# Attention by clusters, then a gated feed-forward layer: a new table of places for the kernel's 2390 tasks

## The chip, the cores and the metric

The kernel runs on one core of a Trainium2 chip. The metric is the device time of one execution in microseconds, lower is better. Names of engines: PE is the matrix engine (TensorE), DVE the vector engine, ACT the scalar engine, POOL the GpSimd engine, SP the engine that does little else than issue DMAs. PEld stands for loading weights into the matrix engine, which overlaps its matmuls.

## The reference: what is computed

Four batches of eight heads, 768 positions, 64 elements per head. Each query and each key belongs to one of 16 clusters of its head, and only pairs of the same cluster attend to each other. The result of all heads goes, as 3072 tokens of 512 elements, through a feed-forward layer with a sigmoid gate, 1536 wide inside:

```python
q_assign = np.argmax(np.einsum('bhsd,hcd->bhsc', q_n, c_n), axis=-1)
k_assign = np.argmax(np.einsum('bhsd,hcd->bhsc', k_n, c_n), axis=-1)
mask = q_assign[:, :, :, None] == k_assign[:, :, None, :]
scores = scale * np.matmul(q, k.transpose(0, 1, 3, 2))
scores = np.where(mask, scores, -1000000000.0)
...
gate = 1.0 / (1.0 + np.exp(-(x @ w_gate)))
val = x @ w_val
return (gate * val @ w_out).astype(np.float32)
```

The inputs and the output are float32.

## The kernel before

**Work.** Heads go in pairs, (batch, pair) from (0,0) to (3,3). For each pair, q and k (tiles `nat`) are loaded, transposed on PE into PSUM (L723) or by DVE (L701), and copied to SBUF as `t32` (L683 on DVE, others on ACT). POOL casts `t32` to fp16 tiles `even` and `odd` (L756). A group of fp32 matmuls of 16 instructions (`scored`, L793 and its like) compares `t32` with the centroids; from it DVE makes a one-hot matrix of each position's cluster, and small transposes (L680) put it as 16 further rows beneath `even` and `odd`. A score matmul (L1113) thus contracts over 80 rows, and the 16 extra ones are the cluster mask. Several score matmuls fill two PSUM banks, ACT takes the exponential of both at once (L1137, into `es`), and value products (L1164) follow. Their 65th column is the sum of a row: DVE takes its reciprocal (L1189) and multiplies (L1194, into `xn`). The result is transposed into the layer's input `x`, either on PE with a cast by DVE (L1202, L1218) or by a transposing DMA from SP (L1222).

**The layer.** A block of tokens goes through the two projections (L1505), ACT's sigmoid, and the gated product on DVE (L1684, into `hT`). From the second batch on the projections are in part replaced by seven products of halves in place of eight (L1583), which need sums of weights (L1486) and evacuations with additions. The output projection is done by seven products as well (L1374), with sums of activations on DVE (L1344) and sums of the weights `wo` (L1272 to L1277). These sums are made once, after the three loads of `wo`, which POOL issues.

**The order.** Nothing runs in the order in which it is written. The program first records 2390 tasks: 1048 for PE, 584 for DVE, 453 for ACT, 107 for POOL, 198 for SP. A task is a small group of instructions of one engine with its dependencies, an assumed duration, and the buffers it takes. `Order.schedule` then plays them through: on each engine, among the tasks that could start within 0.02 us of the earliest one, it takes that with the lowest place (`due`, from the table `PLACES`):

```python
first = min(c[0] for c in cand)
start, t = min(
    (c for c in cand if c[0] <= first + 0.02), key=lambda c: (c[1].due, c[0])
)
```

For DMAs it assumes the time from issue to landing in the table `LANDINGS`. In the same pass it deals out the buffers: `ring` is the pool of eight PSUM banks, and a task gets one of those that are free when the planner believes it to start. So the places set the order of each engine's instructions and also which bank a product lands in, hence for which evacuation it waits. On the chip the engines then run that fixed order, with semaphores between them. A DMA of POOL is issued only when fewer than eight of POOL's are under way; these loads and SP's transposes share the core's 16 DMA engines.

Around the places shown below: `prepare_pair` (L885) records the transposes, copies and casts of a pair, `attend` (L1091) scores to norms, `sum_weights` (L1254) the sums over `wo`, `feed` (L1492) the projections. Their code is the same in both kernels.

Of the kernel before, what the change touches and what calls it, by code (L numbers as in the profile page):

```python
# [17 lines left out]
0 1 10 13 16 2 3 9 12 11 6 15 17 19 20 32 36 4 8 5 14 18 21 23 27 75 68 31 37 40 99 94 43 47 52 215 128 58 163 194  # L18
105 119 221 207 277 259 475 252 501 7 22 24 30 26 25 29 35 41 28 33 38 50 34 39 44 46 42 48 53 57 61 64 65 70 77 86
82 79 45 51 49 55 54 59 56 62 63 112 78 87 76 90 101 113 138 136 144 158 133 124 139 88 97 96 107 106 118 114 129  # L20
131 156 137 147 135 151 160 169 214 191 179 204 185 196 199 117 122 130 140 132 145 150 183 171 229 182 198 195 219
227 235 248 242 257 270 261 275 268 104 110 116 192 172 200 184 253 206 265 228 279 250 287 254 290 285 299 288 305
267 286 295 300 316 323 318 361 368 380 399 330 348 373 403 413 420 407 427 439 433 454 446 336 381 363 342 349 431
441 371 355 448 488 424 521 554 529 535 512 517 539 543 594 598 639 643 558 568 574 605 648 678 647 653 657 663 670
673 654 660 664 675 677 693 685 709 716 695 704 713 787 66 67 69 73 85 71 72 74 80 92 81 83 84 89 100 91 93 95 98
123 142 149 152 102 103 108 153 109 111 115 154 120 121 126 157 125 127 134 159 141 143 155 170 146 148 161 181 189
209 216 162 164 165 166 167 168 173 217 174 175 176 177 178 180 186 218 225 232 237 187 188 190 193 197 238 201 202
203 205 208 239 210 211 212 213 220 241 246 251 255 222 223 224 226 230 256 231 233 234 236 240 258 243 244 245 247
249 266 273 284 310 319 260 262 263 264 269 298 271 272 274 276 278 301 280 281 282 283 289 311 317 321 332 338 459
466 515 506 344 352 347 365 360 370 372 385 353 359 383 392 421 432 426 443 401 410 405 425 434 453 465 472 444 457  # L30
494 499 473 486 485 492 500 509 528 534 536 542 538 546 508 526 516 530 552 560 556 567 291 292 293 294 296 297 302
333 303 304 306 307 308 309 313 334 341 346 350 314 315 320 351 325 327 331 364 328 329 337 366 339 340 345 393 357
358 362 394 367 369 374 397 402 406 462 375 376 377 378 379 382 384 412 386 387 388 389 390 391 395 415 422 428 477
398 400 404 442 408 411 416 450 417 418 423 455 429 430 436 458 437 440 445 460 449 452 461 476 483 487 495 463 467
468 469 470 471 474 493 478 479 480 481 482 484 489 503 507 510 519 523 490 491 496 520 497 498 502 522 504 505 511
525 513 514 518 541 524 527 531 545 532 533 537 547 551 553 557 562 572 577 624 619 570 576 604 618 591 627 626 637
635 642 640 649 622 631 652 668 575 581 579 623 613 621 617 628 655 674 683 690 661 672 671 680 676 687 705 714 692
719 701 724 666 694 686 697 711 723 717 729 573 580 587 612 615 616 620 630 645 578 583 592 602 708 722 727 728 732
# [1783 lines left out]
```

## Time and profile before

| | |
|---|---|
| median of 3 runs | 311.12 us (310.98 to 311.52) |
| the profiled execution | 310.43 us, its span 308.6 us |
| busy: PE, ACT, DVE, POOL | 299.5, 260.1, 248.5, 79.2 us |
| granted clock of PE | 1.00 |

The span goes from the first to the last instruction; the execution is 1.8 us longer. A row of the timeline gives the start of a run of like instructions, the time from the first one's start to the last one's end, engine, line, operation, the tiles that are written and read, the shape, the count, and in brackets how long the engine was idle before it and what ended that. Matmuls are pipelined: 128x512 ones start 0.22 us apart though each lasts longer. The lines of code in the profile after will be higher by one than those before, since the new table is a line longer.

### The profile page before, as it was taken

To read this page: it belongs to the slowest core of one execution; us is meant where nothing else is said; L and a number is where in the kernel's file an instruction comes from. 1 tells how busy PE (TensorE), PEld (TensorE's weight loads), DVE (VectorE), ACT (ScalarE), POOL (GpSimd) and SP (SyncE) were. 2 spreads that over 40 slices of the span, in tenths; PEclk is the share of its full clock that TensorE was granted. 3 is DMA by queue.
4 is the path that set the end of the run, shared out by engine and by line. 5 is a ranking of instruction groups with operands and counts; after the bars stand their busy time and mean duration, and the time that the engine had idled before them with its cause. 6 is when DMAs were issued, how large, how long until landed. Compare 5 with 4: busy or idle time off the path is not lost.

```text
span 308.6 us, 8896 instructions
## 1 busy us (share of the span) xinstructions
PE 299.5 (97%) x3491; PEld 237.5 (77%) x3491; DVE 248.5 (81%) x604; ACT 260.1 (84%) x449; POOL 79.2 (26%) x112
## 2 busy tenths in 40 slices
PE   8999999989999999999999999999999999999995
PEld 3667588744468688977998779886998889878974
DVE  4999996798796696889679979979786839864993
ACT  4798899975539899999999988999999998995841
POOL 4998738751022014600001211370000000010000
PEclk9999999999999999999999999999999999999999
DMA  6999999999457389920376564894210120051003
GB/s 216 376 283 165 177 225 158 149 154 130 76 90 145 71 180 152 150 36 15 81 121 120 97 106 106 184 136 32 68 21 35 29 81 34 3 96 70 0 3 136
DMA packets 97833, 34.79 MB, mean 113 GB/s; under 512 B 83152, under 2 KB 93568, under 8 KB 97792
## 3 DMA queue, kind: packets, MB, share of 16 engines
q1 hardware_dynamic: 72192, 24.57, 35.6%
q0 software_dynamic: 24880, 8.92, 28.9%
q10 hardware_dynamic: 720, 0.75, 0.7%
q8 instruction: 27, 0.44, 0.6%
q14 instruction: 14, 0.11, 0.1%
HBM read 28.87 MB, written 6.29 MB: 114 GB/s over the span
## 4 chain that ended last, share of the span: by engine, by line
PE 71%; ACT 13%; DVE 8%; DMA 4%; issue 2%; ACTq 0%; DVEq 0%
PE ring L1583 19%; PE ring L1374 17%; PE ring L1113 14%; PE ring L1505 10%; PE ring L1164 8%; ACT es L1137 7%; DMA x<-xn 3%; PE ring L793 2%; ACT nat L1621 2%; ACT nat L1602 2%; DVE even L680 2%; DVE t L683 1%; DVE odd L680 1%; DMA out<-in_centroids_dram 1%; ACT p L1602 1%
## 5 line engine op out<-in xcount | busy, mean ns | idle before, releaser
L1137 ACT ACTIVATE es<-ring,nbias 128x768 f16<-128x768 f32 (+1 forms) x189 | 168.9, 939 | 16.4 <-PE ring L1113 10.1
L1164 PEld LDWEIGHTS <-es 128*128 128x128 f16 x1152 | 50.8, 97 | 9.5 <-ACT es L1137 0.8
L1164 PE MATMUL ring<-vp,es 128*128 128x65 f16 x1152 | 55.7, 193 | 0.2 <-ACT es L1137 0.2
L1614 DVE TENSOR_TENSOR nat<-ring,nat 128x384 f32<-128x384 f32 x68 | 36.9, 552 | 17.5 <-PE ring L1583 9.5
L756 POOL CAST even<-t 128x768 f16<-128x768 f32 x24 | 20.9, 876 | 113.9 <-DVE t L701 49.0
L1621 ACT ACTIVATE nat<-nat 128x384 f32<-128x384 f32 x68 | 38.4, 582 | 2.4 <-DVE nat L1614 2.3
L1583 PEld LDWEIGHTS <-wss 128*128 128x128 f16 x408 | 34.5, 98 | 2.2
L1602 ACT COPY nat<-ring 128x384 f32<-128x384 f32 x68 | 34.4, 521 | 2.1 <-PE ring L1583 1.1
L1583 PE MATMUL ring<-nat,wv 128*128 128x192 f16 x272 | 32.9, 246 | 0.0
L1583 PE MATMUL ring<-x,wg 128*128 128x192 f16 x272 | 32.6, 246 | 0.0
L1583 PE MATMUL ring<-nat,wss 128*128 128x192 f16 x272 | 31.9, 246 | 0.0
L1374 PEld LDWEIGHTS <-hT 128*128 128x128 f16 x294 | 27.4, 97 | 5.7 <-DVE hT L1630 0.4
L1374 PE MATMUL ring<-wo,hT 128*128 128x256 f16 x216 | 29.0, 272 | 0.1
L1113 PE MATMUL ring<-even 80*128 80x384 f16 (+2 forms) x120 | 26.4, 294 | 1.1 <-ACT es L1137 0.5
L1113 PE MATMUL ring<-even,odd 80*128 80x384 f16 (+2 forms) x120 | 26.4, 293 | 0.5 <-DVE t L683 0.4
L1113 PE MATMUL ring<-odd 80*128 80x384 f16 x96 | 26.2, 325 | 0.0
L1113 PE MATMUL ring<-odd,even 80*128 80x384 f16 x96 | 25.8, 326 | 0.3 <-ACT es L1137 0.2
L1583 PEld LDWEIGHTS <-wv 128*128 128x128 f16 x272 | 23.5, 97 | 2.4
L1113 PEld LDWEIGHTS <-odd 80*128 80x128 f16 x216 | 18.7, 98 | 7.5 <-issue 4.4
L1113 PEld LDWEIGHTS <-even 80*128 80x128 f16 x216 | 19.0, 98 | 7.0 <-issue 3.2
L1583 PEld LDWEIGHTS <-wg 128*128 128x128 f16 x272 | 23.1, 98 | 1.5
L1505 PE MATMUL ring<-x,wg 128*128 128x256 f16 (+2 forms) x112 | 22.6, 325 | 1.0 <-DMA x<-xn 1.0
(120 smaller groups left out, 519.6 us busy)
## 6 DMA issues: line engine op xcount, KB each, us to landing
out_dram<-out SPq DMA_DIRECT2D x22, 256.0 KB, 2.3
nat<-in_k_dram SPq DMA_DIRECT2D x32, 96.0 KB, 2.9
nat<-in_q_dram SPq DMA_DIRECT2D x32, 96.0 KB, 3.0
odd<-even SPq DMA_DIRECT2D x12, 192.0 KB, 4.2
vp<-in_v_dram POOLq DMA_DIRECT2D x24, 96.0 KB, 5.1
nat<-in_k_dram SPq DMA_DIRECT2D x5, 384.0 KB, 7.2
nat<-in_q_dram SPq DMA_DIRECT2D x5, 384.0 KB, 6.1
nat<-in_v_dram SPq DMA_DIRECT2D x4, 384.0 KB, 7.2
```

The lines of the kernel that those rows point to most:

```text
L680: nc.vector.transpose(to.bitcast(FP), of.bitcast(FP))
L756: nc.gpsimd.tensor_copy(t[:, NM[nm], cols], t32[p, nm].tile[:, cols])
L793: nc.tensor.matmul(out=ps[32 * g : 32 * g + 32, half, :QB], lhsT=cblk[:, 2 * p + half, :], rhs=t32[p, nm].tile[:, half * QB : (half + 1) * ...
L1113: nc.tensor.matmul(out=to, lhsT=kb.tile[0:80, 0, e * QB + j // 2 * 128 : e * QB + (j // 2 + 1) * 128], rhs=qb_.tile[0:80, 1, e * QB + c0 * ...
L1137: i = nc.scalar.activation(to, of, AF.Exp, bias=nbias, scale=D ** -0.5 if quarters(b, p) else scale,).ins
L1164: nc.tensor.matmul(out=av.tile[:, g : g + D + 1], lhsT=es.tile[:, i * N + c * 128 : i * N + (c + 1) * 128], rhs=vp[:, e, j, :], start=firs ...
L1374: nc.tensor.matmul(out=ps[:, lo:hi], lhsT=left_()[:, i], rhs=right(i)[:, lo:hi], start=new and i == 0, stop=i == NFC // 2 - 1, skip_group_ ...
L1505: nc.tensor.matmul(out=ps[:, :N], lhsT=ws[fc // FPG][:, dcc, fc % FPG, :], rhs=xb.tile[:, dcc, :N], start=(dcc == 0), stop=(dcc == NDC - 1),)
L1583: nc.tensor.matmul(out=ps[:, f], lhsT=w_[:, d, f], rhs=x_()[:, d], start=new and not (f or d), stop=d == 1, skip_group_check=True,)
L1602: nc.scalar.copy(held(i), bank(r_))
L1614: lambda: nc.vector.tensor_tensor(held(i), bank(r_), held(i), ALU.add), deps,
L1621: lambda: nc.scalar.activation(held(i), held(i), AF.Tanh, scale=0.5), [m], due_ffn(work), lat=0.16,
```

## The change

Two tables of numbers have other values: `PLACES` and `LANDINGS`. All code is the same, and so are the 2390 tasks, what each computes and what it depends on. Of the places 1889 differ, by 5.7 on average and at most by 106; of the 254 landings some 45 differ by more than 0.3 us.

```diff
--- before.py
+++ after.py
@@ -15,115 +15,116 @@
 PLACES = """
-0 1 10 13 16 2 3 9 12 11 6 15 17 19 20 32 36 4 8 5 14 18 21 23 27 75 68 31 37 40 99 94 43 47 52 215 128 58 163 194
-105 119 221 207 277 259 475 252 501 7 22 24 30 26 25 29 35 41 28 33 38 50 34 39 44 46 42 48 53 57 61 64 65 70 77 86
...
+0 1 9 2 16 3 5 10 11 13 14 15 17 19 20 32 36 4 8 6 12 18 21 23 27 92 97 31 37 40 101 115 43 47 52 165 169 58 178 184
+107 121 225 233 263 268 495 255 502 7 22 24 26 30 25 29 35 41 28 33 38 46 34 39 44 50 42 48 53 57 61 64 65 70 76 78
...
 """
 
 LANDINGS = """
-2.6 3.45 4.13 3.7 4.2 3.45 3.88 4.31 4.74 5.17 5.6 6.03 6.46 6.89 7.1 8.68 11.77 8.87 10.7 15.58 12.84 9.47 10.5
...
+2.6 3.45 4.13 3.7 4.2 3.45 3.88 4.31 4.74 5.17 5.6 6.03 6.46 6.89 7.1 8.677 11.409 7.348 9.688 13.473 16.613 9.04
...
```

(Each table goes on for many lines; they are all numbers of this kind.) What follows shows how instructions move. On PE 410 of 1048 tasks stand at the same position as before, on DVE 243 of 584, on ACT 304 of 453, on POOL 46 of 107, on SP 81 of 198. The largest shift on an engine is 25 tasks on PE, 16 on DVE, 6 on ACT, 8 on POOL and 13 on SP.

**The last pair of the first batch: DVE.** `ohf0` is the one-hot matrix of pair (0,3), `even3` and `odd3` the operands of its scores; the copies into `t320` to `t323` empty the banks of fp32 transposes of a later pair. Before:

```order
L680 STREAM_TRANSPOSE even3_77<-ohf0_92 32x192
L1194 TENSOR_TENSOR xn3_105<-ring_121,rr0_99 128x256
L683 TENSOR_SCALAR t320_70<-ring_121 128x384
L680 STREAM_TRANSPOSE odd3_83<-ohf0_92 32x192
L680 STREAM_TRANSPOSE even3_77<-ohf0_92 32x192
L683 TENSOR_SCALAR t321_71<-ring_121 128x384
L680 STREAM_TRANSPOSE even3_77<-ohf0_92 32x192
L1189 RECIPROCAL rr1_100<-ring_121 128x4
L680 STREAM_TRANSPOSE odd3_83<-ohf0_92 32x192
L683 TENSOR_SCALAR t321_71<-ring_121 128x384
L1194 TENSOR_TENSOR xn0_102<-ring_121,rr1_100 128x256
L683 TENSOR_SCALAR t322_72<-ring_121 128x384 x2
```

and with the change, from the first of the small transposes on:

```order
L681 STREAM_TRANSPOSE even3_77<-ohf0_92 32x192
L1190 RECIPROCAL rr0_99<-ring_121 128x4
L681 STREAM_TRANSPOSE even3_77<-ohf0_92 32x192
L1195 TENSOR_TENSOR xn3_105<-ring_121,rr0_99 128x256
L681 STREAM_TRANSPOSE odd3_83<-ohf0_92 32x192
L681 STREAM_TRANSPOSE even3_77<-ohf0_92 32x192 x2
L681 STREAM_TRANSPOSE odd3_83<-ohf0_92 32x192
L684 TENSOR_SCALAR t320_70<-ring_121 128x384
L1190 RECIPROCAL rr1_100<-ring_121 128x4
L684 TENSOR_SCALAR t320_70<-ring_121 128x384
L1195 TENSOR_TENSOR xn0_102<-ring_121,rr1_100 128x256
L684 TENSOR_SCALAR t321_71<-ring_121 128x384 x2
```

The six small transposes now stand ahead of all copies; the first copy into `t320`, formerly further ahead, is behind them too.

**The same place on PE.** L723 is the group of transposes that those copies empty; the scores with `even3` and `odd3` are the last of the pair. Before:

```order
L1113 MATMUL ring_121<-even3_77 128x256
L1113 LDWEIGHTS even3_77
L1113 MATMUL ring_121<-even3_77 128x256
L1113 LDWEIGHTS odd3_83
L1113 MATMUL ring_121<-even3_77,odd3_83 128x256
L1113 LDWEIGHTS odd3_83
L1113 MATMUL ring_121<-even3_77,odd3_83 128x256
L1113 LDWEIGHTS odd3_83
L1113 MATMUL ring_121<-even3_77,odd3_83 128x256
L723 MATMUL ring_121<-ident_124,nat3_64 128x128 x6
L1113 LDWEIGHTS even1_75
L1113 MATMUL ring_121<-even1_75 128x128
```

and with the change:

```order
L1203 LDWEIGHTS xn0_102
L1203 MATMUL ring_121<-ident16_125,xn0_102 128x128
L1203 LDWEIGHTS xn0_102
L1203 MATMUL ring_121<-ident16_125,xn0_102 128x128
L724 MATMUL ring_121<-ident_124,nat3_64 128x128 x3
L1114 LDWEIGHTS even3_77
L1114 MATMUL ring_121<-even3_77 128x256
L1114 LDWEIGHTS odd3_83
L1114 MATMUL ring_121<-even3_77,odd3_83 128x256
L1114 LDWEIGHTS odd3_83
L1114 MATMUL ring_121<-even3_77,odd3_83 128x256
L1114 LDWEIGHTS odd3_83
```

The last four scores of the pair now stand behind a turn of `xn0` and the last three transposes of `nat3`, for which the planner takes the bank that the second copy into `t321` empties. Before, the transposes stood behind these scores.

**Loads: POOL.** `wo0` and `wo2` are two of the three tiles of the output weights, `vp` the values of a pair, `nat` the quarters of a q or k. Before:

```order
L440 DMA nat3_64<-in_k_dram 32x24x32
L440 DMA nat5_66<-in_q_dram 32x24x32 x2
L440 DMA nat3_64<-in_k_dram 32x24x32
L440 DMA vp4_144<-in_v_dram 128x6x64 x2
L440 DMA wo0_136<-in_moe_w_out_dram 128x4x512
L440 DMA nat3_64<-in_k_dram 32x24x32
L440 DMA wo2_138<-in_moe_w_out_dram 128x4x512
L440 DMA vp0_140<-in_v_dram 128x6x64 x2
```

and with the change:

```order
L441 DMA vp4_144<-in_v_dram 128x6x64 x2
L441 DMA nat4_65<-in_k_dram 32x24x32 x3
L441 DMA nat5_66<-in_q_dram 32x24x32 x3
L441 DMA nat3_64<-in_k_dram 32x24x32 x3
L441 DMA vp0_140<-in_v_dram 128x6x64 x2
L441 DMA wo0_136<-in_moe_w_out_dram 128x4x512
L441 DMA wo2_138<-in_moe_w_out_dram 128x4x512
```

`vp0` now stands ahead of both weight tiles instead of behind them, and `vp4` further ahead of them than before.

**Transposing DMAs: SP.** Before:

```order
L1222 DMA_TRANSPOSE x1_107<-xn2_104 128x1x128
L440 DMA even5_79<-oht0_86 16x768
L440 DMA even4_78<-oht0_86 16x768 x2
L440 DMA even5_79<-oht0_86 16x768
L440 DMA odd4_84<-oht0_86 16x768 x2
L440 DMA odd5_85<-oht0_86 16x768 x2
L1222 DMA_TRANSPOSE x1_107<-xn3_105 128x3x128
L1222 DMA_TRANSPOSE x1_107<-xn0_102 128x1x128
L1222 DMA_TRANSPOSE x1_107<-xn1_103 128x3x128
```

and with the change:

```order
L1223 DMA_TRANSPOSE x1_107<-xn2_104 128x1x128
L1223 DMA_TRANSPOSE x1_107<-xn3_105 128x3x128
L441 DMA even4_78<-oht0_86 16x768 x2
L1223 DMA_TRANSPOSE x1_107<-xn0_102 128x1x128
L441 DMA even5_79<-oht0_86 16x768 x2
L441 DMA odd4_84<-oht0_86 16x768 x2
L441 DMA odd5_85<-oht0_86 16x768 x2
L1223 DMA_TRANSPOSE x1_107<-xn1_103 128x3x128
```

Two of the transposes into `x1` have moved ahead of most of the eight small DMAs; the last one stays behind them.

**The sums over the output weights: DVE.** Before:

```order
L701 STREAM_TRANSPOSE t322_72<-nat3_64 128x384 x2
L1344 TENSOR_TENSOR s120_116<-hT0_108,s110_115 128x768
L1189 RECIPROCAL rr0_99<-ring_121 128x6
L1194 TENSOR_TENSOR xn0_102<-ring_121,rr0_99 128x384
L1275 TENSOR_TENSOR nat7_68<-wo0_136,nat6_67 128x512
L1275 TENSOR_TENSOR nat7_68<-wo1_137,nat6_67 128x512
L1275 TENSOR_TENSOR nat7_68<-wo2_138,nat6_67 128x512
L1684 SCALAR_TENSOR_TENSOR hT1_109<-gt0_110,ring_121 128x512
L1277 TENSOR_TENSOR nat8_69<-wo0_136,nat7_68 128x512
L1684 SCALAR_TENSOR_TENSOR hT1_109<-gt1_111,ring_121 128x512
L1486 TENSOR_TENSOR wv1_134<-wg1_131,wv1_134 128x2x256
L1684 SCALAR_TENSOR_TENSOR hT1_109<-gt0_110,ring_121 128x512
```

and with the change:

```order
L1685 SCALAR_TENSOR_TENSOR hT1_109<-gt0_110,ring_121 128x512
L1273 TENSOR_TENSOR nat6_67<-wo1_137 128x512
L1274 TENSOR_TENSOR wo1_137<-wo1_137 128x2x256
L1273 TENSOR_TENSOR nat6_67<-wo2_138 128x512
L1274 TENSOR_TENSOR wo2_138<-wo2_138 128x2x256
L1276 TENSOR_TENSOR nat7_68<-wo0_136,nat6_67 128x512
L1276 TENSOR_TENSOR nat7_68<-wo1_137,nat6_67 128x512
L1276 TENSOR_TENSOR nat7_68<-wo2_138,nat6_67 128x512
L1278 TENSOR_TENSOR nat8_69<-wo0_136,nat7_68 128x512
L1278 TENSOR_TENSOR nat8_69<-wo1_137,nat7_68 128x512
L1278 TENSOR_TENSOR nat8_69<-wo2_138,nat7_68 128x512
L1685 SCALAR_TENSOR_TENSOR hT1_109<-gt1_111,ring_121 128x512
```

The nine instructions over `wo0` to `wo2` now stand in one row between two gated products into `hT1`, without the sums and the copy-transposes (`L1344`, `L701`) that stood between them.

Elsewhere tasks of PE, DVE and ACT trade places with neighbours. One such place is near the middle of the program, where six matmuls of the output projection (L1374) now stand ahead of a score that they followed.

205 rows, old and new, of tables (LANDINGS, PLACES) are left out of this document.

## The prediction

> **What bounds the kernel now.** I read the page first, then busy time by stretches, and then the engines' timelines wherever TensorE stood still. The page:
>
> ```profile
> span 308.6 us, 8896 instructions
> PE 299.5 (97%) x3491; PEld 237.5 (77%) x3491; DVE 248.5 (81%) x604; ACT 260.1 (84%) x449; POOL 79.2 (26%) x112
> PE 71%; ACT 13%; DVE 8%; DMA 4%; issue 2%; ACTq 0%; DVEq 0%
> ```
>
> PE is busy 97% of the span and carries 71% of the chain of waits. No instruction is removed here, so only time in which PE waits can be won, and any new wait is lost. The stretches tell where that time is (columns: us, then busy us and instruction count of PE, PEld, DVE, ACT and POOL, the granted clock, the DMA share, GB/s):
>
> ```profile
> 26.50:33.00 6.50, 5.51 (x77) 4.02 (x76) 6.12 (x17) 5.20 (x6) 3.99 (x6) 1.00 1.36 113
> 36.00:62.00 26.00, 25.48 (x338) 20.15 (x330) 20.97 (x58) 24.42 (x38) 17.58 (x24) 1.00 1.26 183
> 60.00:64.00 4.00, 2.98 (x29) 1.51 (x27) 3.72 (x6) 2.77 (x5) 3.08 (x4) 1.00 1.60 175
> 64.00:145.00 81.00, 81.00 (x869) 57.62 (x868) 66.70 (x154) 65.54 (x107) 17.50 (x21) 1.00 0.79 108
> ```
>
> PE lacks 1.0 us of work in 26.5 to 33, 1.0 us in 60 to 64, and nothing in 64 to 145. So the change decides itself at three places: the last pair of the first group (27 to 36 us), the weight loads and transposes around 50 to 70 us, and one wait at 145 us. Everywhere else PE is dense: a shuffle there can cost and hardly win.
>
> **Place 1: copies behind transposes, 27 to 36 us.** DVE feeds PE here, and its timeline shows in which order:
>
> ```profile
> 27.68 0.37 DVE L680 STREAM_TRANSPOSE even<-ohf 32x192 f32<-32x192 f32 x1
> 29.03 0.55 DVE L683 TENSOR_SCALAR t<-ring 128x384 f32<-128x384 f32 x1
> 30.41 0.56 DVE L683 TENSOR_SCALAR t<-ring 128x384 f32<-128x384 f32 x1
> 32.01 0.56 DVE L683 TENSOR_SCALAR t<-ring 128x384 f32<-128x384 f32 x1
> 32.60 0.42 DVE L1194 TENSOR_TENSOR xn<-ring,rr 128x256 f16<-128x256 f32 x1
> 32.94 1.94 DVE L683 TENSOR_SCALAR t<-ring 128x384 f32<-128x384 f32 x4
> ```
>
> Copies (L683, 0.55 us) empty the banks of PE's fp32 transposes; the small transposes (L680, 0.37 us) make the operands of the scores. Today they alternate. The changed order has all six L680 first, then the copies. Up to the second copy into t321 DVE has the same set of tasks behind it as today up to the norm at 32.60, which ends at 33.02. DVE is busy 6.12 of 6.50 us in this stretch, so that copy ends at about 33.1, whatever the order. On PE and ACT:
>
> ```profile
> 31.02 0.38 PE L1113 MATMUL ring<-even,odd 80*128 80x256 f16 x2 [0.44 <-DVE t L683]
> 32.04 0.50 PE L1113 MATMUL ring<-even,odd 80*128 80x256 f16 x3
> 32.63 1.00 PE L723 MATMUL ring<-ident,nat 128*128 128x128 f32 x6
> 34.99 0.49 PE L1113 MATMUL ring<-odd,even 80*128 80x384 f16 x2
> 35.41 1.50 PE L793 MATMUL ring<-t,cblk 128*32 128x384 f32 x16
> 30.44 1.11 ACT L1137 ACTIVATE es<-ring,nbias 128x1024 f16<-128x1024 f32 x1 [0.95 <-PE ring L1113]
> 31.91 4.61 ACT L1137 ACTIVATE es<-ring,nbias 128x1024 f16<-128x1024 f32 x5 [0.35 <-PE ring L1113]
> ```
>
> Today the pair's last scores are issued by 32.4, and the second exponential of the row of five takes them at about 32.9 (31.91 + 1.0). The third starts at 34.0 and ends at 34.9; at 34.99 PE goes on with the scores that need its bank, and the cluster scores (L793) follow at 35.41. In the new order those last four scores stand behind three L723 transposes, for which the planner dealt the bank that the second t321 copy empties. So: 33.1 + 0.06 for the semaphore + three transposes at 0.14 (0.84 us from 32.63 to the next group, for six) + four scores at 0.11 and 0.16 more until the last has drained = 34.15 for the exponential. That is 1.2 later than 32.9. The next exponential and the bank follow by the same amount, so L793 starts at about 36.5 instead of 35.41: **+1.1 us**. Behind it PE is dense (25.48 of 26.00 us in 36 to 62), so it isn't won back. Bounds: +0.5 if the lead of a few tenths that the new order has from 12 to 28 us lets the copies end before 32.6; +1.5 if every one of the copies waits for PE's transposes in turn.
>
> **Place 2: the x transpose and the weights of the last layer, 50 to 70 us.**
>
> ```profile
> 61.07 0.60 PE L1505 MATMUL ring<-x,wg 128*128 128x512 f16 x2
> 62.69 1.47 PE L1505 MATMUL ring<-x,wg 128*128 128x512 f16 x6 [1.02 <-DMA x<-xn]
> 50.83 4.01 SPq L1222 DMA_TRANSPOSE x<-xn  x3
> 51.96 0.78 POOL L440 DMA_DIRECT2D wo<-in_moe_w_out_dram  x1
> 53.43 0.87 POOL L440 DMA_DIRECT2D wo<-in_moe_w_out_dram  x1
> 54.18 1.65 POOL L440 DMA_DIRECT2D vp<-in_v_dram  x2
> x<-xn SPq DMA_TRANSPOSE x1, 9.2
> wo<-in_moe_w_out_dram POOLq DMA_DIRECT2D x2, 512.0 KB, 9.4
> DMA to landing us min/median/max: 8.1/9.4/10.8
> DMA to landing us min/median/max: 11.2/11.4/11.6
> DMA to landing us min/median/max: 2.7/2.7/2.7
> ```
>
> (The last five: the transpose issued last, the two wo loads in the stretch 51 to 54, their own landings, those of the two vp loads from 54.18 on, and, for comparison, a transpose issued at 91.9.) The transpose issued at 53.4 lands at 62.6 and releases PE: 62.69 − 61.07 − 2 × 0.22 (the x6 group's spacing) = 1.18 us lost. Issue plus landing gives wo 51.96 + 8.1 = 60.1 and 53.43 + 10.8 = 64.2, vp 54.18 + 11.2 = 65.4 and about 55.0 + 11.6 = 66.6: things land in the order of issue, across both queues, while the backlog lasts. One vp therefore costs 1.2 us, and one wo, from the landing before it at about 57.1, at most 2.9.
>
> The change issues vp ahead of both wo, and two of three x transposes ahead of SP's eight small moves. The last transpose then has no wo ahead of it and one vp more: 62.6 − 2.9 + 1.2 = 60.9; with both vp ahead 62.1. PE would want it at 61.07 − 0.7 (work moved behind it) + 0.4 (two matmuls) + 1.1 (place 1) = 61.9. The wait goes: **−1.18 us**, bound −0.6 if x lands at 62.5. By the Trainium skill ("DMA: Bandwidth & Descriptors", section "Queues, rings and completion order") each DMA engine takes turns between the queues it has work for, a packet at a time; by that the SP transpose would not stand behind POOL's loads at all. The 9.2 us against 2.7 speak against it, though not finally: that reading is rival 3.
>
> The price: the two wo land later, at about 60.1 + 2 × 1.2 + 1.3 (a quarter of nat, the last transpose) = 63.8 and 64.2 + 2.4 = 66.6. DVE sums over them (L1272 to L1277) hold back what is behind them in the queue:
>
> ```profile
> 61.05 1.87 DVE L1272 TENSOR_TENSOR nat<-wo 128x512 f16<-128x512 f16 x1
> 62.95 0.42 DVE L1273 TENSOR_TENSOR wo<-wo 128x512 f16<-128x512 f16 x1
> 68.37 1.08 DVE L1275 TENSOR_TENSOR nat<-wo,nat 128x512 f16<-128x512 f16 x3
> 69.38 0.68 DVE L1684 SCALAR_TENSOR_TENSOR hT<-gt,ring 128x512 f16<-128x512 f32 x1
> 70.31 0.68 DVE L1684 SCALAR_TENSOR_TENSOR hT<-gt,ring 128x512 f16<-128x512 f32 x1
> ```
>
> In the new order the first gated product (L1684) stands behind the two sums of the first wo: 63.8 + 0.8 = 64.6, and, with the rows that come before it in time, 65.5. The second stands behind everything: 66.6 + 0.8 (the last pair of sums) + 6 × 0.34 (three L1275 take 1.08) = 69.4, and ends at 70.1. PE asks for the banks that these two empty at about 66 and 69.5 (two scores of batch 1 that the planner put onto them): 0 to 0.3, and 0.2 to 0.6: **+0.5 us**. Bounds: 0, if the loads drain while the queue is not full (PE then never asks too early), and +1.3, if the first L1272 takes its 1.87 us beside POOL's casts again and the sums follow 0.8 later.
>
> **Place 3: 145 us.**
>
> ```profile
> 145.42 0.32 PE L1113 MATMUL ring<-even 80*128 80x384 f16 x1 [0.19 <-ACT es L1137]
> ```
>
> This score waited for ACT; six matmuls of the output layer (L1374) now stand ahead of it. They fill the gap of 0.35 us (0.19 idle, and the fill and drain around it): **−0.35**; 0 if ACT then is behind at the next score too.
>
> **All else** (over a thousand tasks moved by up to 25 places on PE, 16 on DVE, 6 on ACT) I price at 0: in 64 to 145 us PE already has 81.00 of 81.00, and the banks' releases have a stage of slack. The cover is ACT's and DVE's idle time there (65.54 and 66.70 of 81): if an order asks a bank one task too early, it costs one evacuation, 0.4 to 0.7 us. Bounds ±0.6.
>
> **Sum:** 1.1 − 1.18 + 0.5 − 0.35 = +0.07 us. The profiled execution took 310.43 us (1.8 of it around its span of 308.6) and the runs' median is 311.12, 0.7 above it; the sum is made on the profile, and put on the median it gives **311.2 us**.
>
> **The rivals.**
>
> 1. *Slower: DVE's queue head.* Sums that wait for wo block the gated products, so PE stalls at 66 and 69.5 by the full +1.3, and place 1 costs +1.5. 311.12 + 1.5 + 1.3 − 1.18 = 312.7. For it: at 62 to 70 DVE has hardly any idle time (3.72 of 4.00). Against: a wo has landed in 8.1 us. It decides once the second wo lands after 66.9.
> 2. *Faster: the start loses little and the gains are all real.* Place 1 +0.5, wait for x gone, wo in time, 145 us gained: 311.12 + 0.5 − 1.18 − 0.35 = 310.1. For it: the new order is ahead by some tenths before 28 us. Against: DVE has 0.4 us of idle time in 26.5 to 33.
> 3. *The x transpose isn't held back by what is issued before it* but by its own queue and the load on the engines. It then lands at about 62.6 as today. PE, asking at 61.9, still loses 0.7: 311.12 + 1.1 − 0.5 + 0.5 − 0.35 = 311.9. For it: the transpose's 9.2 us and the loads' 8.1 to 10.8 are alike, which a shared backlog gives in any case. Against: landings in order of issue over two queues.
>
> **Chances.** Forecast 0.44 (own range 310.4 to 311.9), rival 1 0.17, rival 2 0.25, rival 3 0.14. A measurement of this kernel tells a change from none at about 0.2%, 0.62 us here: below 310.50 is faster, above 311.74 slower. Faster: rival 2 and 0.05 of the forecast, 0.30. Slower: rival 1, 0.09 of rival 3, 0.05 of the forecast, 0.31. Same: 0.39. The range from 309.6 to 312.8 leaves out the outer parts of rivals 1 and 2 and what the ±0.6 adds to them.
>
> **What would show it.** Right: DVE's first t320 copy behind the six small transposes at about 30.5, L793 at 36.2 to 36.7 (35.41 now), no wait for x at 61 to 63, wo landing at 63 to 67 and two short PE waits between 65 and 70, no ACT wait at 145. From 75 us to the end the distance between the two kernels would stay as it is. Wrong: L793 before 36.0; a new PE wait over 0.5 us behind 75 us; x landing at 62.6 or later; a gap at 66 to 70 over 1 us. The step I trust least is place 1, because one bank decides it.

## The result

| | before | with the change |
|---|---|---|
| median of 17 runs | 311.12 us (310.40 to 314.09) | 309.89 us (309.38 to 310.94) |
| profiled execution, its span | 310.43, 308.6 us | 309.38, 307.6 us |

The ratio is 0.9944, with a 95% interval of 0.9923 to 0.9965: the change makes the kernel faster by about half a per cent. The forecast was 311.2 us, no change to be measured. The wide range (309.6 to 312.8) held the time; the forecast's own (310.4 to 311.9) did not, and a change that is clear of the noise was not foreseen.

### The profile after

All lines of code are higher by one. The page, with the chain of waits last:

```profile
span 307.6 us, 8905 instructions
PE 299.2 (97%) x3491; PEld 237.5 (77%) x3491; DVE 249.3 (81%) x604; ACT 259.0 (84%) x449; POOL 79.2 (26%) x112
PE 89%; ACT 4%; DVE 3%; DMA 2%; issue 1%; ACTq 0%; SPq 0%
```

PE's work is the same, and its share of the chain has grown from 71 to 89%. The chain follows whatever came last at each step, so such a shift says that waits have left it, not how long they were. The stretches say that (columns as in the prediction):

```profile
26.50:33.00 6.50, 5.57 (x79) 4.56 (x76) 6.15 (x17) 4.38 (x5) 4.58 (x6) 1.00 1.01 152
36.00:62.00 26.00, 25.70 (x328) 20.04 (x321) 21.08 (x58) 23.41 (x37) 19.50 (x26) 1.00 1.48 185
60.00:64.00 4.00, 4.00 (x24) 2.11 (x22) 3.93 (x8) 3.53 (x7) 4.00 (x6) 1.00 1.41 221
64.00:145.00 81.00, 81.00 (x882) 57.65 (x880) 65.61 (x152) 65.47 (x109) 14.89 (x18) 1.00 0.73 103
```

PE is busy for all of 60 to 64 us, where it lacked 1.0. In 26.5 to 33 it lacks 0.9, about as before. Place 1, PE's timeline from the last scores to the cluster scores, and ACT's exponentials:

```profile
30.23 0.55 PE L724 MATMUL ring<-ident,nat 128*128 128x128 f32 x3 [0.49 <-DVE t L684]
32.15 0.55 PE L724 MATMUL ring<-ident,nat 128*128 128x128 f32 x3
32.62 0.27 PE L1114 MATMUL ring<-even 80*128 80x256 f16 x1
34.42 0.33 PE L1114 MATMUL ring<-even 80*128 80x128 f16 x3 [0.62 <-ACT es L1138]
35.42 1.50 PE L794 MATMUL ring<-t,cblk 128*32 128x384 f32 x16
25.41 3.24 ACT L1138 ACTIVATE es<-ring,nbias 128x1024 f16<-128x1024 f32 x3
33.25 3.49 ACT L1138 ACTIVATE es<-ring,nbias 128x1024 f16<-128x1024 f32 x4 [0.69 <-PE ring L1114]
```

The row of three exponentials starts at 25.41 instead of 26.28, so the new order arrives 0.87 us ahead (0.23 of it because the first score starts earlier in this execution, at 10.36 instead of 10.59), and the cluster scores (now L794) start at 35.42, as before (35.41). The lead is used up. Place 2, PE at the projection that had waited, and the landings of the last x transpose (from 52.2) and of the two wo loads (from 52.9 and 53.6):

```profile
60.79 1.03 PE L1506 MATMUL ring<-x,wg 128*128 128x512 f16 x4
61.66 1.03 PE L1506 MATMUL ring<-x,wv 128*128 128x512 f16 x4
L1223 SPq DMA_TRANSPOSE x<-xn x1: 1211/1211/1211, 52.2 to 52.2; - x1
DMA to landing us min/median/max: 5.2/5.2/5.2
L441 POOL DMA_DIRECT2D wo<-in_moe_w_out_dram x2: 760/760/761, 52.9 to 53.6; - x2
DMA to landing us min/median/max: 7.7/8.6/9.6
```

The transpose lands at 57.4, more than three microseconds before PE asks. The wo loads land at 60.6 and 63.2; before it was 60.1 and 64.2.

### The profile page after: what moved, and what is told of

It reads as the page before. It is cut to its first block, busy times and chain, and to the rows that moved or that the text cites. A ratio compares the mean times of both kernels' runs of the same rounds, so it can differ in the third digit from the quotient of the medians.

```text
span 307.6 us, 8905 instructions
## 1 busy us (share of the span) xinstructions
PE 299.2 (97%) x3491; PEld 237.5 (77%) x3491; DVE 249.3 (81%) x604; ACT 259.0 (84%) x449; POOL 79.2 (26%) x112
## 2 busy tenths in 40 slices
DMA packets 97833, 34.79 MB, mean 113 GB/s; under 512 B 83152, under 2 KB 93568, under 8 KB 97792
## 4 chain that ended last, share of the span: by engine, by line
PE 89%; ACT 4%; DVE 3%; DMA 2%; issue 1%; ACTq 0%; SPq 0%
PE ring L1584 25%; PE ring L1114 19%; PE ring L1375 18%; PE ring L1506 11%; PE ring L1165 10%; ACT es L1138 3%; PE ring L794 3%; DMA nat<-in_q_dram 1%; PE ring L902 1%; DVE hT L1631 1%; DMA out<-in_centroids_dram 1%; DVE t L684 1%; PE ring L942 1%; DVE even L681 0%; ACT t L909 0%
## 5 line engine op out<-in xcount | busy, mean ns | idle before, releaser
L1165 PE MATMUL ring<-vp,es 128*128 128x65 f16 x1152 | 56.6, 193 | 0.0
L1622 ACT ACTIVATE nat<-nat 128x384 f32<-128x384 f32 x68 | 37.3, 575 | 1.9 <-DVE nat L1615 1.9
L1584 PE MATMUL ring<-nat,wv 128*128 128x192 f16 x272 | 32.6, 246 | 0.0
L1114 PE MATMUL ring<-odd 80*128 80x384 f16 x96 | 26.5, 325 | 0.1
```

Source lines behind the costliest of these rows:

```text
L1114: nc.tensor.matmul(out=to, lhsT=kb.tile[0:80, 0, e * QB + j // 2 * 128 : e * QB + (j // 2 + 1) * 128], rhs=qb_.tile[0:80, 1, e * QB + c0 * ...
L1165: nc.tensor.matmul(out=av.tile[:, g : g + D + 1], lhsT=es.tile[:, i * N + c * 128 : i * N + (c + 1) * 128], rhs=vp[:, e, j, :], start=firs ...
L1584: nc.tensor.matmul(out=ps[:, f], lhsT=w_[:, d, f], rhs=x_()[:, d], start=new and not (f or d), stop=d == 1, skip_group_check=True,)
L1622: lambda: nc.scalar.activation(held(i), held(i), AF.Tanh, scale=0.5), [m], due_ffn(work), lat=0.16,
```

## The experiments

Each experiment is the kernel before, the changed one, or a mixture of the two, with an order written out in place of the planner's. The two tables hold a list of tasks and a list of PSUM banks, and `run` plays them back:

```diff
-        for t, at in zip(self.tasks, places):
-            t.due = at
-        order = self.schedule()
+        order, banks, count = [self.tasks[i] for i in which], iter(banks), {tag: 0 for tag in self.bufs}
+        for t in order:
+            for b in t.acq:
+                b.slot = next(banks) if b.tag in self.ANY else count[b.tag] % self.bufs[b.tag]
+                count[b.tag] += 1
         for t in order:
             t.emit()
```

A task can thus be moved alone, without the planner answering with other moves elsewhere. Lines of code are numbered as in the kernel before. The ratios are against runs of the kernel before that were taken together with the experiment's; its medians there were 311.06, 311.39, 311.35 and 311.02 us.

One number of each profile disturbs the comparison: when the first score starts. It is 10.36 to 10.79 us in thirteen of the fourteen traces and 11.97 in p3_before. There PE ran at half its pace between 7 and 9 us, as the same eight matmuls show, in the kernel before and in p3_before:

```profile
6.87 0.96 PE L1054 MATMUL ring<-t,cblk 128*32 128x384 f32 x8 [0.45 <-DVE cblk L536]
7.28 1.93 PE L1054 MATMUL ring<-t,cblk 128*32 128x384 f32 x8
```

In the trace of p3_before the record of the full granted clock begins at 10.0 us, in the others at 3.4 to 6.3 (the page counts the time ahead of that record as full). So the traces are compared by stretches between tasks that stand in all of them: the first score (10.59 us in the kernel before), the sixth of the exponentials of 1024 columns (28.39), the cluster scores (35.41), the projection at 70.68, and the last product but a few (298.67). Up to the cluster scores, the projection and the last product both orders have done the same PE work. Up to the exponential they have not: the new order has three fp32 transposes (L723) fewer done by then, p3_before three more than the old one. For the start of the kernel the first two columns are therefore to be added up. The lengths, in us:

| kernel | first score to exponential | to cluster scores | to projection | to the end |
|---|---|---|---|---|
| before | 17.79 | 7.02 | 35.28 | 227.99 |
| changed | 17.18 | 7.88 | 34.52 | 227.72 |
| s1_new (new to 35 us) | 17.39 | 7.87 | 36.24 | 228.07 |
| s12_new (new to 75 us) | 17.21 | 7.88 | 34.73 | 227.93 |
| s1_old (new from 35 us) | 18.16 | 7.05 | 34.79 | 227.86 |
| o_turns_first | 17.88 | 7.37 | 35.71 | 227.99 |
| p3_before | 18.37 | 6.39 | 34.90 | 227.64 |
| vp_first | 18.09 | 7.05 | 34.72 | 228.09 |
| xt_first | 18.03 | 7.04 | 34.21 | 228.10 |
| vp_xt_first | 18.23 | 7.04 | 34.15 | 228.08 |
| x_late | 17.95 | 7.02 | 36.53 | 228.00 |
| wo_late | 17.94 | 7.88 | 36.85 | 227.63 |
| best1 | 17.79 | 7.03 | 34.26 | 227.70 |
| best3 | 17.82 | 7.02 | 36.47 | 227.78 |

The second and the fourth column repeat to within 0.03 and 0.25 us wherever the order is the same. The first varies by several tenths; why was not traced.

### The order in parts: s1_new, s12_new, s1_old

**s1_new** takes the new order to the cluster scores, the old one from there.

> The new order up to the fp32 cluster scores at 35.4 us (L793), the old order behind them, played back from a written list (some tasks behind the seam get other banks). Theory A (the gain lies in the wait for x at 62.7 us; the start is worth nothing by 35.4 us): cluster scores at 35.4 (35.2 to 35.7), the wait of about 1.2 us for x is still there, time within 0.3% of before, 310.5 to 311.8 us. Theory B (the start brings the gain and what follows only keeps it): 309.9 us or less, PE ahead of before from 36 us on. Theory C, my forecast of place 1 (+1.1): cluster scores at 36.5, time 312.2.

Measured: 312.18 us, ratio 1.0040 (1.0016 to 1.0064). The cluster scores start at 35.85. The start does not bring the gain. The time is that of theory C and above the range of theory A, but not for the reason of theory C: the first two stretches are together 0.45 us longer than in the kernel before (25.26 against 24.81), not 1.1. The larger part, 0.96 us, is in the third stretch, where the wait for x has grown. SP issued the last transpose at 55.06 instead of 53.41 and it landed at 64.05; why SP was later was not traced:

```profile
64.10 1.47 PE L1505 MATMUL ring<-x,wg 128*128 128x512 f16 x6 [1.83 <-DMA x<-xn]
```

**s12_new** takes the new order to 75 us.

> The new order up to the cluster scores at 75 us, the old one behind. Theory A: x is there when PE asks, the distance of about 0.75 us to before stands at 76 us and is kept to the end, without the 0.3 us that the new order wins at 145 us: 310.2 us, 0.9 less than before. Theory D (the gain is made by the order behind 75 us): time of before, 311.1.

Measured: 310.20 us, ratio 0.9964 (0.9937 to 0.9992). Most of the gain stands by 75 us. Behind it the changed kernel is shorter by another 0.2 us (last column).

**s1_old** takes the old order to the cluster scores and the new one from there.

> The old order up to the cluster scores at 35.4 us, the new one behind. If the new start costs 0.4 us (cluster scores at 35.85 with the usual first loads, in two kernels with the new start, 35.4 in the old): 309.5 to 309.7, better than both kernels. If the seam (three score pairs in other banks) costs more than that: 310.0 to 310.5. If the new start were the gain: 310.8 or more.

Measured: 310.13 us, ratio 0.9972 (0.9948 to 0.9997), much like the changed kernel. So the gain can be had without the new start. That the new start costs 0.4 us, which was one expectation, does not show in the time.

### Place 1: o_turns_first, p3_before

**o_turns_first** moves only DVE's small transposes of pair (0,3):

```diff
 L1194 TENSOR_TENSOR xn_105<-ring,rr_99 128x256
+L680 STREAM_TRANSPOSE odd_83<-ohf_92 32x192
+L680 STREAM_TRANSPOSE even_77<-ohf_92 32x192 x2
+L680 STREAM_TRANSPOSE odd_83<-ohf_92 32x192
 L683 TENSOR_SCALAR t_70<-ring 128x384
-L680 STREAM_TRANSPOSE odd_83<-ohf_92 32x192
-L680 STREAM_TRANSPOSE even_77<-ohf_92 32x192
 L683 TENSOR_SCALAR t_71<-ring 128x384
-L680 STREAM_TRANSPOSE even_77<-ohf_92 32x192
 L1189 RECIPROCAL rr_100<-ring 128x4
-L680 STREAM_TRANSPOSE odd_83<-ohf_92 32x192
 L683 TENSOR_SCALAR t_71<-ring 128x384
```

> The kernel before with one thing changed: on DVE the small transposes of pair (0,3) stand ahead of the two copies between them (L680 ahead of L683), as in the new order; PE, banks and DMAs as before. My forecast's mechanism (the copies behind the transposes hold up PE, with no lead to pay for it): cluster scores at 36.1 to 36.6 instead of 35.4, time +0.7 to +1.1, about 312.0. Rival (DVE's order there doesn't matter, because PE waits for the last of all copies anyway): 35.4 and 311.1.

Measured: 311.95 us, ratio 1.0038 (1.0006 to 1.0070); the second stretch is longer by 0.35 us, not by 0.7 to 1.1. PE's timeline shows the mechanism and why its price is lower:

```profile
31.84 0.38 PE L1113 MATMUL ring<-even,odd 80*128 80x256 f16 x2 [1.20 <-DVE t L683]
32.38 0.49 PE L1113 MATMUL ring<-even,odd 80*128 80x256 f16 x3
32.71 0.82 PE L723 MATMUL ring<-ident,nat 128*128 128x128 f32 x6
35.80 1.50 PE L793 MATMUL ring<-t,cblk 128*32 128x384 f32 x16
```

PE waits 1.20 us for the late copy instead of 0.44. But in the old order three more short waits came behind that one, ahead of the rows at 32.04 and 32.63 and of this one:

```profile
31.43 0.50 PE L1113 MATMUL ring<-even 80*128 80x256 f16 x3
```

They are gone: the small transposes are done, and the scores follow each other. Most of the new wait replaces old ones. The time as a whole rose by more than 0.35, because the third stretch is 0.43 longer as well: at 61.16 us PE waits 0.72 for a norm on DVE, which had to wait for a transposing DMA that landed at 60.46, behind the first wo. That belongs to place 2.

**p3_before** is the changed kernel with pair (0,3) in the old order from 27 to 35 us, with the banks dealt anew there.

> The changed kernel, but pair (0,3) from 27 to 35 us in the old order of PE and DVE (copies between the small transposes), with banks dealt anew there. If the new order there costs the lead of 0.75 us that it has at 27 us: cluster scores at 34.7 to 34.9, time 309.2. If the lead can't be used whatever the order (banks, exponentials): 35.4 and 309.9. If the banks at the two seams cost more: 35.6 to 36.2, 310.2 to 310.7.

Measured: 310.43 us, ratio 0.9973 (0.9943 to 1.0002). From the first score to the cluster scores it takes 24.76 us, against 25.06 in the changed kernel and 24.81 in the kernel before. In these single traces the old order at this place keeps about 0.3 us of what the new one loses there. The third stretch is 0.4 longer than in the changed kernel and takes that away; that the newly dealt banks are the cause is likely and not shown. As a whole this kernel was not faster than the changed one. (Its profiled execution, the one with the slow start, took 311.01.)

### Place 2: vp_first, xt_first, vp_xt_first, x_late, wo_late

**vp_first** is the kernel before with five POOL loads in another order:

```diff
 L440 DMA vp_144<-in_v_dram 128x6x64 x2
+L440 DMA nat_64<-in_k_dram 32x24x32
+L440 DMA vp_140<-in_v_dram 128x6x64 x2
 L440 DMA wo_136<-in_moe_w_out_dram 128x4x512
-L440 DMA nat_64<-in_k_dram 32x24x32
 L440 DMA wo_138<-in_moe_w_out_dram 128x4x512
-L440 DMA vp_140<-in_v_dram 128x6x64 x2
```

> The kernel before with five POOL DMAs in another order: the two loads of vp0 and a quarter of nat3 ahead of both wo; all else as before. If transfers land in the order of issue over both queues: the x transpose issued last lands at 59.5 to 61 us instead of 62.6, no or little wait for x at 61 to 63, wo at about 62.5 and 65.5; PE gains up to 1.2 there, less what DVE's sums over wo, which now wait 1.5 us at 61, cost (0 to 1.0). If SP's queue takes turns with POOL's: x at 62.6 and the wait as before.

Measured: 309.76 us, ratio 0.9958 (0.9939 to 0.9977). In the profiled execution the last transpose was issued at 53.48, just behind the first wo (53.08), and landed with it at 62.4, so a part of the wait is left:

```profile
62.40 1.47 PE L1505 MATMUL ring<-x,wg 128*128 128x512 f16 x6 [0.46 <-DMA x<-xn]
```

The landing of 59.5 to 61 that I had expected was missed by that 0.4 us of issue time. By the medians, five moved loads give as much as the whole new table. The trace shows less (third stretch 34.72, the changed kernel 34.52); its execution took 310.24, half a microsecond more than the median.

**xt_first** moves two x transposes ahead of the small DMAs on SP (and the norm that one of them needs by one place on DVE):

```diff
 L1222 DMA_TRANSPOSE x_107<-xn_104 128x1x128
+L1222 DMA_TRANSPOSE x_107<-xn_105 128x3x128
 L440 DMA even_79<-oht_86 16x768
-L440 DMA even_78<-oht_86 16x768 x2
+L440 DMA even_78<-oht_86 16x768
+L1222 DMA_TRANSPOSE x_107<-xn_102 128x1x128
+L440 DMA even_78<-oht_86 16x768
...
-L1222 DMA_TRANSPOSE x_107<-xn_105 128x3x128
-L1222 DMA_TRANSPOSE x_107<-xn_102 128x1x128
 L1222 DMA_TRANSPOSE x_107<-xn_103 128x3x128
```

> The kernel before with SP's order changed: two of the three late x transposes ahead of the small DMAs of the one-hot rows (and one norm on DVE earlier for it); POOL as before. In order of issue: those two land at 50 to 53, the last one is still issued behind the first wo and lands at 60.5 to 61.5; the wait shrinks from 1.18 to 0 to 0.3 us. If the landing is set by SP's queue alone: about 58, no wait. If by POOL's backlog alone: 62.6, wait as before.

Measured: 310.16 us, ratio 0.9958 (0.9930 to 0.9987). The two transposes land at 50.5 and 52.8, the last one, behind both wo (51.1 and 52.6), at 61.7. PE's eight matmuls run almost through:

```profile
61.22 2.02 PE L1505 MATMUL ring<-x,wg 128*128 128x512 f16 x8
```

They take 2.02 us. At the usual 0.22 from one start to the next it would be 1.9. The third stretch is shorter by 1.07 us than before.

**vp_xt_first** has both.

> Both of these together in the kernel before. Theory A (the removed wait is the gain, and the DMA order makes it): x lands before 60, no wait, end 0.7 to 1.2 us earlier than before: 310.0 to 310.4. Theory E (the sums over wo give the gain back): no wait, but PE waits between 65 and 70 us, time 311.

Measured: 311.23 us, ratio 1.0003 (0.9981 to 1.0024), though by its trace it is as short as xt_first (third stretch 34.15) and no PE wait shows between 65 and 70 us. Most of its ten runs lie between 310.9 and 311.5, the profiled one took 309.98. The difference between these runs and the profiled one has not been explained. A slow start as in the trace of p3_before costs 1.2 to 1.6 us up to the first score and would be of that size, but no trace of such a run of this kernel exists. Theory A stands by the stretches, not by this time.

**x_late** moves one POOL load of the kernel before, so that both wo stand ahead of the last transpose:

```diff
 L440 DMA wo_136<-in_moe_w_out_dram
+L440 DMA wo_138<-in_moe_w_out_dram
 L440 DMA nat_64<-in_k_dram 32x24x32
-L440 DMA wo_138<-in_moe_w_out_dram
 L440 DMA vp_140<-in_v_dram 128x6x64 x2
```

> The kernel before with one POOL DMA moved: the second wo load ahead of the quarter of nat3 and so ahead of the last x transpose in the order of issue. All else as before. In order of issue: that transpose lands at 63.8 to 64.5 us instead of 62.6, PE's wait there grows from 1.2 to 2.4 to 3 us, time +1.2 to +1.8: 312.5 to 313.2. In turns between the queues: 62.6 and 311.2. On the granted clock: in 13 of 79 executions of the kernel before, the clock was 0.992 to 0.994 and the time 2 to 4 us longer, in none of 77 of the kernels without the wait. If the wait itself brings that about, those executions become frequent here, a third or more, at 315 and above; if not, they stay at about a sixth.

Measured: 312.04 us, ratio 1.0014 (0.9981 to 1.0047). PE's wait and SP's transposes:

```profile
64.02 1.47 PE L1505 MATMUL ring<-x,wg 128*128 128x512 f16 x6 [2.28 <-DMA x<-xn]
50.21 5.15 SPq L1222 DMA_TRANSPOSE x<-xn  x3
```

The last transpose was issued at 52.8 and landed at 64.0, and the third stretch is longer by 1.25 us, as expected from the order of issue. Taken alone this trace is weak evidence: in s1_new, with POOL's old order, the last transpose landed at 64.05 too. But all traces together say that a load on POOL's queue holds up a transpose on SP's. From issue to landing the last transpose took 5.1 to 6.6 us in the six with no wo issued ahead of it (the changed kernel, wo_late, s12_new, s1_old, p3_before, best3), and 8.3 to 11.2 us in the eight with one or two wo ahead. SP's own order does not make that difference: in xt_first, vp_xt_first and best1 the other two transposes stand ahead of the small DMAs as in the changed kernel, and the last one took 8.3 to 8.6.

The order of issue is not a strict rule, though. In this trace the transpose before the last, issued at 51.51, just behind the second wo (51.42), landed at 60.1, and that wo at 63.7. In s1_new the last transpose landed before two vp that had been issued 1.3 and 2.1 us ahead of it (64.05 against 64.8 and 65.6). The Trainium skill, "DMA: Bandwidth & Descriptors", section "Queues, rings and completion order", says that a DMA engine takes turns, a packet at a time, between the queues it has work for; by that rule alone a load on POOL's queue would not move the transpose. The landings above do not agree with that reading for these two queues, nor with a strict common order.

The time of the ten runs rose by 0.7 us against the kernel before beside them (311.35), less than the trace says; that interval is wide. Three of the ten had a granted clock of 0.993 to 0.995 and took 313.2 to 314.3 us, not 315 and above; on that see the last section.

**wo_late** is the changed kernel with both wo behind one more quarter of nat:

```diff
 L440 DMA vp_140<-in_v_dram 128x6x64 x2
+L440 DMA nat_65<-in_q_dram 32x24x32
 L440 DMA wo_136<-in_moe_w_out_dram 128x4x512
 L440 DMA wo_138<-in_moe_w_out_dram 128x4x512
-L440 DMA nat_65<-in_q_dram 32x24x32 x4
+L440 DMA nat_65<-in_q_dram 32x24x32 x3
```

> The changed kernel with both wo loads issued one place later on POOL, behind a quarter of nat4, which can only be issued at 56 us: wo issued at 56.8 and 57.5 instead of 52.9 and 53.7, landing at about 62.5 and 65.3 instead of 60.6 and 63.2. My forecast's price for late sums (DVE's row of sums holds back the gated products, PE asks for their banks at 66 and 69.5): 0.5 to 1.3 us between 64 and 70 us, 310.4 to 311.2. If DVE has slack there: no PE wait up to 70 us, 309.9.

Measured: 312.36 us, ratio 1.0036 (1.0010 to 1.0062), 2.5 us above the median of the changed kernel. The wo loads were issued still later than expected (58.2 and 59.0) and landed at 64.4 and 67.9. DVE and PE:

```profile
64.40 0.42 DVE L1272 TENSOR_TENSOR nat<-wo 128x512 f16<-128x512 f16 x1 [1.82 <-DMA wo<-in_moe_w_out_dram]
67.93 0.42 DVE L1272 TENSOR_TENSOR nat<-wo 128x512 f16<-128x512 f16 x1 [1.23 <-DMA wo<-in_moe_w_out_dram]
68.73 1.09 DVE L1275 TENSOR_TENSOR nat<-wo,nat 128x512 f16<-128x512 f16 x3
69.73 1.09 DVE L1277 TENSOR_TENSOR nat<-wo,nat 128x512 f16<-128x512 f16 x3
70.74 0.68 DVE L1684 SCALAR_TENSOR_TENSOR hT<-gt,ring 128x512 f16<-128x512 f32 x1
72.16 1.02 PE L1505 MATMUL ring<-x,wv 128*128 128x512 f16 x4 [2.21 <-ACT gt L1672]
```

This is the mechanism that my forecast priced: the row of sums waits for wo, the gated product (L1684) behind it is late, and PE stops. The wait is put down to ACT's sigmoid, which itself stood behind that product. In the changed kernel the second wo lands at 63.2 and PE has no wait at all up to 70 us; here PE loses 2.33 (third stretch 36.85 against 34.52). This execution is 0.92 us later from the cluster scores on, so the landing at 67.9 corresponds to 67.0 in the changed kernel's time. s12_new stops at the same matmul, by 0.22: its second wo lands at 65.3, 64.9 in the changed kernel's time. Between the two the landing is 2.1 us later and the loss 2.1 us larger. So the loss grows one for one, and by an estimate from these two traces it sets in at a landing of about 64.6.

### Towards a better version: best1, best3

**best1** takes the old order with SP's order of xt_first and the second wo behind vp0, and from 71 us the new order.

> The old order up to 71 us with SP's order of xt_first and the second wo load behind vp0, the new order behind 71 us. By the stretches of the traces: start as before (35.4 us, no loss), no wait for x (-1.1), the new order's gain behind 77 us (-0.5), without the stalls of 0.4 us that the new order has at 38 to 42: 309.4 to 309.6, below both kernels. If the seam or the first loads cost 0.3 to 0.5 us: 309.9 to 310.1, the same as the changed kernel.

Measured: 310.20 us, ratio 0.9964 (0.9932 to 0.9996). By its trace it is the shortest of all (286.78 us from the first score to the last product but a few, the changed kernel 287.29), and five of its twelve runs took 309.0 to 309.3, which no run of the others reached. But the others of the twelve range up to 314.1, and so the median is no better than that of the changed kernel. Its last transpose lands at 61.8, about when PE asks for it.

**best3** was to take that edge away: vp0 ahead of both wo, the last transpose ahead of two small DMAs.

> As best1 (old order up to 71 us, new order behind), with the loads of vp0 and a quarter of nat3 ahead of both wo loads, and the last x transpose ahead of two of SP's small DMAs, so that it is issued at about 52 us, ahead of the first wo load at 53. In order of issue it lands at 57.5 to 59 us, 3 us before PE asks, with the sums over wo (landing at 62.2 and 64.5) inside DVE's slack. Then the executions in which x came late in best1 are gone: median 309.2 to 309.5, all below 311. If PE's wait for x has nothing to do with best1's slower executions: median 310.0 to 310.3 as there.

Measured: 311.72 us, ratio 1.0014 (0.9990 to 1.0038). The transpose landed at 58.7 and PE had no wait for it. But to issue it earlier I had to move what it needs, and value products came ahead of their exponentials on PE, which was not meant:

```profile
51.09 0.35 PE L1164 MATMUL ring<-vp,es 128*128 128x65 f16 x6 [0.99 <-ACT es L1137]
```

The third stretch grew by 2.2 us, so the version is no better. What it does show is its spread: 311.3 to 312.4 in twelve runs.

## Why the prediction was wrong

**Place 1, +1.1 us: wrong, about +0.25.** The failed step is "DVE is busy 6.12 of 6.50 us in this stretch, so that copy ends at about 33.1, whatever the order". DVE did have the same tasks behind it, and one copy more, but it did not come to them at the same time. One piece of its lead shows in its rows, where the same instruction takes half the time, of before and of after:

```profile
26.58 1.06 DVE L669 TENSOR_TENSOR ohf<-t,mx 128x384 f16<-128x384 f32 x1
```

```profile
25.89 0.54 DVE L670 TENSOR_TENSOR ohf<-t,mx 128x384 f16<-128x384 f32 x1
31.08 1.01 DVE L684 TENSOR_SCALAR t<-ring 128x384 f32<-128x384 f32 x2
```

This instruction, the one-hot matrix, ended at 26.43 instead of 27.64, 1.2 us earlier, where I had put a lead of "a few tenths": 0.5 by its own duration, 0.2 by the earlier first score of this execution; the other 0.5 is left for the order up to there and for what differs between executions. The second copy into t321 (the last row's second) ended at 32.09, not 33.1. So the last scores started at 32.62 and the exponential at 33.25 instead of 34.15. The order of the copies does have a price, as o_turns_first shows (+0.35 in the second stretch), and the lead pays most of it. From the first score to the cluster scores the two kernels take 24.81 and 25.06 us; over all the traces it is 24.8 to 25.3 in the old order, and in the new one 25.1 to 25.3 in three and 25.8 in wo_late. My bound of +0.5 "if the lead lets the copies end before 32.6" named the right condition, and the time went beyond it.

**Place 2, the wait for x, −1.18 us: right.** PE's wait went entirely. The landing was 57.4 instead of the 60.9 of the forecast, which had kept the old time of issue and the old queue: SP issued the transpose at 52.2 (53.4 before), and the other two x transposes had landed by 52.3. That a backlog of POOL's loads holds up SP's transpose is borne out by moving either queue (vp_first, xt_first and the landings under x_late). My "things land in the order of issue, across both queues" is true of the trace that I read, but not of all: transposes overtook loads in x_late and s1_new.

**Place 2, the sums over wo, +0.5 us: wrong, 0.** The failed step is the landing, "64.2 + 2.4 = 66.6". I added the two vp to the old time and did not take out what had gone from the queue in front of the second wo: two x transposes and a quarter of nat, which in the new order had been issued and had landed before 57 us. It landed at 63.2. The consequence was described rightly, as wo_late shows, but it needs a landing of about 64.6 or later. (In rival 1, the "3.72 of 4.00" given for 62 to 70 us is DVE's busy time in 60 to 64.)

**Place 3, −0.35 us: the wait went, the time was not won.** The score at 145 us follows its predecessors without a wait:

```profile
144.44 0.82 PE L1375 MATMUL ring<-nat,s 128*128 128x256 f16 x6
145.10 0.33 PE L1114 MATMUL ring<-even 80*128 80x384 f16 x1
```

But take the distance between the two kernels where PE has done the same matmuls in both. It is 0.75 us at the projection (70.68 in the kernel before), 1.01 at 133.9, 0.51 at 141.0, 0.98 at 145.4 and 1.02 at the end. What is won at 145 was lost between 134 and 141, where the new order has small stops of its own, two of them (0.13 and 0.10 us) for exponentials. The 0.27 us by which the changed kernel is shorter behind 70 us had come by 134.

**All else, 0: wrong by about +0.4 between 36 and 60 us, and about −0.27 behind 70.** The third stretch of the changed kernel is only 0.76 us shorter, though the wait of 1.18 is gone. In xt_first, with the old order there, it is 1.07. The new order has two small stops of its own between 41 and 42 us, 0.1 and 0.3 us long, a score at 41.06 and a projection at 41.85; both wait for banks that exponentials free:

```profile
40.50 0.60 PE L1506 MATMUL ring<-x,wv 128*128 128x256 f16 x4
41.06 0.33 PE L1114 MATMUL ring<-even 80*128 80x128 f16 x3
41.39 0.35 PE L1165 MATMUL ring<-vp,es 128*128 128x65 f16 x6
41.85 0.60 PE L1506 MATMUL ring<-x,wg 128*128 128x256 f16 x4
```

**The sum.** By the stretches of the two traces: −0.61 and +0.86 in the start, −0.76 in the middle, −0.27 behind, together −0.78; the span is 1.02 shorter, since the first score came 0.23 earlier, and the median moved by −1.23. The forecast had +1.1, −0.68, and −0.35. So it failed by two costs that did not come, +1.1 for the start and +0.5 for the sums, and these hid the one large gain that it had right. The rival that came nearest was the second, with the gains real and wo in time. That it came so near (310.1) is partly luck: its +0.5 for the start was too high, and it had neither the +0.4 in the middle nor the loss ahead of 145 us. Rival 1 was the right mechanism with the wrong landing time. Rival 3 fell with the landing at 57.4, and its mechanism with the landings under x_late.

## What to carry to other kernels

To say when a transfer lands under a backlog, write down the whole queue anew in the order of issue, over all queues, with what leaves it as well as what joins it. Here that is a first estimate: a transpose landed up to 3.6 us ahead of a large load issued just before it. A busy engine in one stretch does not fix when its tasks end: its start in that stretch must be followed from where the two orders part. And a wait that PE has for one late transfer may be had by moving a handful of issues: here, by the medians, five loads did as much as a table of 2390 places.

## What was not expected

The kernel before has executions with a mean granted clock of 0.992 to 0.995, which take 312 to 316 us: 15 of the 108 that ran beside the experiments. The changed kernel has none in 17, and vp_first, xt_first, vp_xt_first, s12_new, s1_old, p3_before and best3, all with little or no wait for x, have none in 72. Kernels in whose traces PE waits at place 2 have them: 3 of 10 in x_late, 4 of 10 in wo_late, 2 of 10 in o_turns_first, 1 of 10 in s1_new, though also 1 of 12 in best1, which hardly waits. That a wait of PE brings on the lower clock is thus likely and not shown: none of the traces is of such an execution, the clock in the stretches read around the wait (before, x_late, wo_late) is 1.00, and best3 has none although PE waits 0.99 us at 51. Part of the change's gain in the runs beyond that in the traces may be this.

The mean clock does not tell of a slow start: the execution of p3_before that was traced has a mean of 1.0. How often executions start so is not known. It is a possible source of the runs about a microsecond above the others that several of these kernels have at a mean clock near 1.

One instruction of DVE (L669) took 1.06 us in the kernel before and 0.54 in the changed one. In the one POOL has a cast under way from 26.38 to 27.22, in the other none after 25.77:

```profile
26.38 0.84 POOL L929 CAST even<-t 64x768 f16<-64x768 f32 x1
```

```profile
24.17 1.60 POOL L930 CAST odd<-t 64x768 f16<-64x768 f32 x2
```

The same pairing stands in xt_first (1.07, cast at 26.51) and in s1_new (0.54, no cast after 25.3). That the cast makes the instruction longer is what this suggests; no run moves the cast alone.
